# Hashed attention and a feed-forward layer on one core: projections asked for first, one key copy on VectorE, the first pair's values of one half in one stretch, features first in all its scores but one

## The chip, the cores and the metric

The kernel runs on one core of a Trainium2 chip. The metric is the device time of one execution in microseconds (us). Before the change it is 849.15 us, the median of three runs (848.68 to 849.31). Five engines work side by side, each through its own instructions in order: TensorE (PE, with its weight loads listed as PEld), VectorE (DVE), ScalarE (ACT), GpSimd (POOL) and SyncE (SP). SP and ACT also issue the DMA transfers; such issues are listed as SPq and ACTq.

## The reference

The first part is attention over 4 batches of 8 heads, 768 positions, 64 numbers per head, in which a query sees only the keys of its own hash bucket. The second is a feed-forward layer on 3072 tokens with 512 and 2048 features.

```python
q_bits = (einsum('bhsd,dk->bhsk', q, proj) > 0)      # 6 bits; the same for k
mask = q_bucket[:, :, :, None] == k_bucket[:, :, None, :]
scores = where(mask, scale * (q @ k.T), -1e9)
attn = exp(scores - max); attn = attn / (sum(attn) + 1e-9)
out = attn @ v                                       # heads side by side: x, 3072 x 512
h = x @ w_in
y = (h * sigmoid(1.702 * h)) @ w_out
```

## The kernel before, in words

The attention works through 16 pairs of heads (`pairs`, n = 0 to 15; j = 0, 1 is the head in the pair). For a pair, q and k are brought into a layout with the 64 numbers of each head on the partitions (`own`). The mask comes from a second, small product: the 6 hash bits of each key and query are turned into bf16 "features" (`feats`), whose product is large and negative wherever two bits differ. A tile of scores is 128 keys by 384 queries for both heads; it is the sum in PSUM of the f32 product of k and q and of the bf16 product of the features. ScalarE takes the exponential of the tile (`weigh`, L484) into `es`. `values` (L540) multiplies v by these tiles, with 12 matmul instructions for three key tiles and 24 for six; the trace has two records for each f32 matmul. The sums of the weights are formed on GpSimd (`add_low`, L525) and VectorE (`add_high`, L535 and L538).

The queries of a pair are in two halves (c = 0, 1) and its keys in six tiles, three `low` and three `high`. All this is written out by hand: four engines (`ORDERED`, L18) execute in the order of the source, and the fetches on SP keep their program order through `load` (L344).

Pair 0 is special. `first_pair` (L373) issues the DMAs of k, q and proj, builds the hash weights on VectorE (`hash_weights`, L126 to L136, which need proj), runs five matmuls on an idle tile, transposes k and q on PE (`turned`, L395 to L401, two query or key columns of 64 at a time), copies the results from PSUM into `own` by ScalarE or VectorE (`placed`, L403, L405), projects (`bits`, L407 to L412: a matmul at L410 and a VectorE instruction at L411 that writes the features) and leaves the second half of the features to `second` (L425), which is called as `rest()` after the first three score tiles. That second half holds the features of the keys from 384 on and of the second half of the queries. Where `second` projects, k's projection and q's stand one after the other on PE, into one PSUM tile, ahead of both VectorE instructions.

From pair 1 on q and k are fetched in another layout (`fetch`, L347), transposed by VectorE (`turn`, L432, L435), hashed in one go (`hashed`, L454, L460), and the features go from `featured` (L463, L465) by ten small DMAs of 16 rows into `feats`. From pair 2 on (`BY_PARTS`, L334) the scores are made of three terms (`scores_of_four`, L499, L514), for which `exchange` (L437) swaps partition blocks by four DMAs and `copied` (L478) repeats the features by two. `measure` (L445, L450) squares and sums q and k on ScalarE. `place` and `in_turn` (L310 to L317) hand out four PSUM places; the first pair's score tiles use three of them by the list `slots` (L620). `scores` (L486) makes the tiles of pairs 0 and 1; the order of its two terms is set at L492 and L493. The lines L614 to L651 are the hand-written order for pair 0 and the preparations of pairs 1 to 3.

After the attention the feed-forward part runs as nested products of sums of blocks (L847 to L1455); the change does not touch it.

Of the kernel before, what the change touches and what calls it, by code (L numbers as in the profile page):

```python
# [38 lines left out]
def kernel(  # L39
# [17 lines left out]
    nc = tc.nc  # L57

    loader = [nc.sync]
    B, H, S, D = q.shape  # L60
# [23 lines left out]
    pj = const.tile([P, NB], F32, name="pj")  # L84
# [25 lines left out]
    for i, x in enumerate("kq"):  # L110
# [7 lines left out]
        for c in range(2):  # L118
            r0 = D * i + 32 * c
# [41 lines left out]
    for x in (0x3FFFFFFF, 0xFF800000):  # L161
        m = const.tile([P, 1], U32, name=f"mask_{x:x}")
# [131 lines left out]
    def attention(ff):  # L294
# [4 lines left out]
        with actx:  # L299
# [10 lines left out]
            def place(i):  # L310
                return (sps if i % 4 else ends).tile([P, 2, 512], F32, tag=f"s{i % 4}", name="s")
# [32 lines left out]
            def load(out, in_):  # L344
                return tc.keep_in_program_order(nc.sync.dma_start(out=out, in_=in_))

            def fetch(n, name):  # L347

                b, hp = pairs[n]
                if n in (1, 3):  # L350

                    b1, hp1 = pairs[last - 1 - "kq".index(name)]
                    x = xT[:, hp1, b1 * S : (b1 + 1) * S].rearrange("p (s i) -> p s i", i=32)
                else:
                    x = ld.tile([P, S // 32, 32], F32, tag=name, name=name)
                raws[n, name] = x
                src = {"k": k, "q": q}[name]
                for j in range(2):
                    rows = src[b, 2 * hp + j].rearrange("(s p) (a i) -> a p s i", p=32, i=32)
                    for a in range(D // 32):  # L360
                        r0 = D * j + 32 * a
                        load(x[r0 : r0 + 32], rows[a])

            def fetch_v(n):
                b, hp = pairs[n]
                x = vts[n] = ld.tile([P, 2, T, D], F32, tag="v", name="v", bufs=2)
                heads = v[b, 2 * hp : 2 * hp + 2]
                if n:
                    load(x.rearrange("p j t d -> p (j t) d"), heads.rearrange("j (t p) d -> p (j t) d", p=P))
                else:  # L370
                    load(x.rearrange("p j t d -> p j (t d)"), heads.rearrange("j (p t) d -> p j (t d)", p=P))

            def first_pair():  # L373


                b, hp = pairs[0]
                x = {}
                for name, src, queues in (("k", k, (nc.sync, nc.scalar)), ("q", q, (nc.scalar, nc.scalar))):
                    raw = raws[0, name] = ld.tile([P, S // 32, 32], F32, tag=name, name=name)
                    x[name] = raw.rearrange("p s i -> p (s i)").rearrange("p (j t d) -> p j t d", j=2, d=D)  # L380
                    for j, queue in enumerate(queues):
                        queue.dma_start(out=x[name][:, j], in_=src[b, 2 * hp + j].rearrange("(p t) d -> p t d", p=P))
                    if name == "k":
                        for j in range(2):
                            nc.sync.dma_start(out=pj[D * j : D * (j + 1)], in_=proj)
                    xts[0, name] = own[0][:, "kq".index(name)]

                nc.scalar.activation(const.tile([1, 1], F32, name="first"), ones[0:1, 0:1], Act.Exp)
                warm = place(3)
                for _ in range(5):  # L390
                    nc.tensor.matmul(warm[:, 0], idle[:, 0:P], idle, start=True, stop=True)
                hash_weights()


                def turned(name):  # L395
                    tp = in_turn()
                    for j in range(2):
                        for i in range(GT):
                            two = x[name][:, j, 2 * i : 2 * i + 2, :].rearrange("p t d -> p (t d)")
                            nc.tensor.transpose(tp[:, j, i * P : (i + 1) * P], two, ident)  # L400
                    return tp  # L401

                def placed(name, tp, c, moves):  # L403
                    for j, move in enumerate(moves):
                        move(xts[0, name][D * j : D * (j + 1), c * HS : (c + 1) * HS], tp[D * c : D * (c + 1), j, 0:HS])  # L405

                def bits(name, c, h):  # L407
                    cols = slice(c * HS, (c + 1) * HS)
                    h = h[:, 0:HS]
                    nc.tensor.matmul(h, pf0[name].rearrange("p j d -> p (j d)"), xts[0, name][:, cols], start=True, stop=True)  # L410
                    return lambda: nc.vector.tensor_scalar(feats[0][name][:, cols], h, above0[name][:, 0:1], FEAT[name],  # L411
                                                           op0=Alu.is_gt, op1=Alu.mult)  # L412

                act, dve = nc.scalar.copy, nc.vector.tensor_copy
                tk = turned("k")
                placed("k", tk, 0, (act, act))
                tq = turned("q")
                placed("q", tq, 0, (act, dve))
                bits("k", 0, in_turn()[:, 0])()
                placed("k", tk, 1, (act, dve))  # L420
                bits("q", 0, in_turn()[:, 0])()
                placed("q", tq, 1, (act, dve))
                measure(0, "k")

                def second():  # L425
                    at = place(3)
                    for f in [bits(x, 1, at[:, i]) for i, x in enumerate("kq")]:
                        f()

                return second  # L430
# [6 lines left out]
            def exchange(n):  # L437

                for j in range(2):
                    for i in range(2):  # L440
                        r0, r1 = D * j + 32 * i, D * j + 32 * (1 - i)
                        dma = load(other[n % 3][r0 : r0 + 32], own[n % 3][r1 : r1 + 32])
                return dma

            def measure(n, name):  # L445

                x = raws[n, name]
                i = 2 * n + "kq".index(name)
                junk = xT[:, HP - 1, (B - 1) * S : B * S].rearrange("p (s i) -> p s i", i=32)
                nc.scalar.activation(junk, x, Act.Square, accum_out=sizes[:, i : i + 1])  # L450
# [35 lines left out]
            def scores(n, c, kts, slots=None):  # L486
                qT, kT, qf, kf = xts[n, "q"], xts[n, "k"], feats[n % 2]["q"], feats[n % 2]["k"]
                cols = slice(c * HS, (c + 1) * HS)
                for kt in kts:
                    ps = in_turn() if slots is None else place(slots.pop(0))  # L490
                    keys = slice(kt * P, (kt + 1) * P)
                    terms = ((kf, qf), (kT, qT))  # L492
                    for at, (a, m) in enumerate(terms if n else terms[::-1]):  # L493
                        for j in range(2):
                            hs = slice(D * j, D * (j + 1))
                            nc.tensor.matmul(ps[:, j, 0:HS], a[hs, keys], m[hs, cols], start=at == 0, stop=at == 1)  # L496
                    weigh(n, c, kt, ps)
# [42 lines left out]
            def values(n, c, kts, at):  # L540
                av, vt = at[:, 0 : HS + 1], vts[n]
                avs[n, c] = av
                for t in kts:
                    row = t if n else 2 * (t % GT) + t // GT
                    for j in range(2):
                        for d in range(0, D, 32):
                            nc.tensor.matmul(av[D * j + d : D * j + d + 32, :], vt[:, j, row, d : d + 32], es[c][:, t, j, :],  # L547
                                             start=(t == 0), stop=(t == T - 1))
# [71 lines left out]
            slots = [2, 0, 1] * 5  # L620
# [2 lines left out]
            measure(0, "q")  # L623
            fetch(2, "q")
            add_low(0, 0)
            at = place(3)
            scores(0, 0, high, slots)
            for x in "kq":
                turn(1, x)
                measure(1, x)  # L630
            values(0, 0, low, at[:, 0])
            for x in "kq":
                fetch(3, x)
            scores(0, 1, low, slots)
            add_high(0, 0)
            add_low(0, 1)
            for x in "kq":
                turn(2, x)
                measure(2, x)
            values(0, 0, high, at[:, 0])  # L640
            hashed(1, place(slots.pop(0))[:, 0])
            unload(0, 0)
            behind = exchange(2)
            whole(featured(1, behind))
            fetch_v(1)
            scores(0, 1, high, slots)
            add_high(0, 1)
            at = place(3)
            values(0, 1, every, at[:, 0])
# [807 lines left out]
    def whole(steps):  # L1457
        for _ in steps:
            pass
# [49 lines left out]
```

## Time and profile before

| | |
|---|---|
| median of three runs | 849.15 us |
| the profiled execution | 848.73 us |
| its span, first to last instruction | 846.9 us |
| PE busy | 838.0 us (99%) |
| VectorE busy | 673.8 us (80%) |
| ScalarE busy | 337.6 us (40%) |
| GpSimd busy | 366.6 us (43%) |
| score tiles of pairs 0 and 1 end | about 40 us |
| first scores of pair 2 | 45.37 us |

Instructions carry the line of the kernel that made them. A row of the timeline has the start, the length, the engine, the line, the operation, the tile written and those read, the shape and how many were merged; in brackets stand the time that the engine had been idle and what ended that. A PE row's length includes the time in which its last results drain, so rows of PE overlap; the distance from start to start is what a product costs. A waits row names the engine and line that waited, what it waited for, the total in us, how often and the longest. The row with "DMA to landing" has the least, median and greatest time from the issue of a transfer to its landing.

### The profile page before, as it was taken

How to read it: one execution, taken by the hardware profiler on the slowest of the kernel's cores; microseconds unless marked ns; L12 is line 12 of the kernel's file. 1: busy time of each engine (PE TensorE's matmuls, PEld its weight loads, DVE VectorE, ACT ScalarE, POOL GpSimd, SP SyncE). 2: the span in 40 equal slices, each digit the busy share in tenths (PEclk: the TensorE clock that was granted, in tenths of full speed). 3: DMA queues.
4: the chain of work that ended last, by engine and by line, in shares of the span. 5: the costliest groups of instructions: out<-in, count | busy, mean ns of one | idle time of the engine just before them, and what ended most of it. 6: DMA issues, size and time to landing. Idle time of an engine off the chain costs nothing.

```text
span 846.9 us, 14955 instructions
## 1 busy us (share of the span) xinstructions
PE 838.0 (99%) x5644; PEld 519.2 (61%) x5644; DVE 673.8 (80%) x1068; ACT 337.6 (40%) x552; POOL 366.6 (43%) x321
## 2 busy tenths in 40 slices
PE   8999999999999999999999999999999999999996
PEld 4444444444444444566666666545888888888885
DVE  5478888887888985788888788577998977797776
ACT  6766766767676634443444344433000000000000
POOL 4433443334344359996844487578655000000000
PEclk9999999999999999999999999999999999999999
DMA  8687666677773104345555546587754685467524
GB/s 150 117 164 159 156 132 142 141 153 148 155 158 94 50 2 173 149 170 203 218 199 193 211 174 224 198 292 265 263 192 156 193 255 193 156 199 248 197 103 101
DMA packets 165197, 144.92 MB, mean 171 GB/s; under 512 B 124224, under 2 KB 139712, under 8 KB 159872
## 3 DMA queue, kind: packets, MB, share of 16 engines
q1 hardware_dynamic: 154640, 112.11, 47.4%
q10 hardware_dynamic: 10480, 31.81, 11.1%
q8 instruction: 45, 0.74, 0.4%
q14 instruction: 32, 0.26, 0.1%
HBM read 79.69 MB, written 50.33 MB: 154 GB/s over the span
## 4 chain that ended last, share of the span: by engine, by line
PE 98%; POOL 1%; DVE 1%; ACT 0%; issue 0%; ACTq 0%; POOLq 0%; DVEq 0%
PE product L1229 30%; PE product L900 23%; PE s L547 15%; PE s L514 15%; PE small L970 6%; PE product L970 3%; PE s L496 2%; PE s L460 1%; PE s L569 1%; PE s L410 0%; POOL feat L337 0%; DVE feat L411 0%; ACT c L915 0%; DVE own L405 0%; DVE v L918 0%
## 5 line engine op out<-in xcount | busy, mean ns | idle before, releaser
L484 ACT ACTIVATE e<-s 128x768 f32<-128x768 f32 x192 | 143.4, 811 | 48.9 <-PE s L514 43.9
L547 PE MATMUL s<-e,v 128*32 128x385 f32 x1536 | 131.1, 488 | 0.0
L525 POOL TENSOR_TENSOR t_x<-e 128x768 f32<-128x768 f32 x32 | 60.5, 1891 | 136.4 <-ACT e L484 136.4
L900 PE MATMUL product<-xT,w_in_sb 128*128 128x512 f32 x216 | 100.0, 593 | 0.1
L547 PEld LDWEIGHTS s<-e,v 128*32 128x32 f32 x1536 | 46.6, 109 | 79.3 <-issue 62.2
L900 PE MATMUL product<-t_x,s_in 128*128 128x512 f32 x192 | 89.4, 592 | 0.0
L514 PE MATMUL s<-s_in 32*128 32x384 f32 x912 | 87.8, 481 | 0.0
L525 POOL TENSOR_TENSOR t_x<-t_x,e 128x768 f32<-128x768 f32 x32 | 55.2, 1724 | 43.5 <-ACT e L484 42.1
L538 DVE TENSOR_TENSOR acc<-acc,e 128x768 f32<-128x768 f32 x63 | 70.1, 1112 | 2.3
L1265 ACT COPY u<-product 128x256 f32<-128x256 f32 x20 | 7.4, 372 | 158.4 <-PE product L1229 125.2
L900 PEld LDWEIGHTS product<-xT,w_in_sb 128*128 128x128 f32 x216 | 40.9, 190 | 35.8 <-issue 32.5
L514 PEld LDWEIGHTS s<-s_in 32*128 32x128 f32 x912 | 43.8, 185 | 23.4 <-issue 2.2
L900 PEld LDWEIGHTS product<-t_x,s_in 128*128 128x128 f32 x192 | 36.5, 190 | 29.7 <-issue 26.9
L514 PE MATMUL s<-own 32*128 32x384 f32 x432 | 44.3, 482 | 0.0
L465 DVE TENSOR_SCALAR f<-s,above,weight 128x384 bf16<-128x384 f32 x15 | 10.2, 677 | 39.8 <-PE s L569 33.9
L918 DVE TENSOR_TENSOR u<-product,u 128x256 f32<-128x256 f32 (+1 forms) x60 | 28.4, 485 | 15.6 <-PE product L970 12.9
L1229 PE MATMUL product<-raw_g,xT 128*128 128x256 f32 x152 | 35.1, 379 | 0.0
L535 DVE SCALAR_TENSOR_TENSOR acc<-t_x,e 128x768 f32<-128x768 f32 x31 | 29.3, 945 | 6.3 <-POOL t_x L525 3.5
L231 POOL TENSOR_TENSOR v<-c,v 128x1024 f32<-128x1024 f32 (+1 forms) x15 | 32.4, 2159 | 1.0
L230 POOL TENSOR_TENSOR u<-v,u 128x1024 f32<-128x1024 f32 (+1 forms) x11 | 23.9, 2169 | 20.4 <-ACT v L915 15.6
L918 DVE TENSOR_TENSOR v<-product,v 128x512 f32<-128x512 f32 x24 | 16.5, 688 | 20.0 <-PE product L900 20.0
L1229 PEld LDWEIGHTS product<-raw_g,xT 128*128 128x128 f32 x152 | 28.9, 190 | 3.9
(297 smaller groups left out, 1770.7 us busy)
## 6 DMA issues: line engine op xcount, KB each, us to landing
raw_g<-g_dram SPq DMA_DIRECT2D x20, 1024.0 KB, 5.1
s_in<-g_dram SPq DMA_DIRECT2D x20, 1024.0 KB, 5.1
g_dram<-c ACTq DMA_DIRECT2D x18, 512.0 KB, 2.9
raw<-in_moe_w_out_dram ACTq DMA_DIRECT2D x16, 512.0 KB, 3.7
raw<-in_moe_w_in_dram ACTq DMA_DIRECT2D x15, 512.0 KB, 3.8
s_in<-own SPq DMA_DIRECT2D x36, 192.0 KB, 4.0
v<-in_v_dram SPq DMA_DIRECT2D x16, 384.0 KB, 4.1
k<-in_k_dram SPq DMA_DIRECT2D x52, 96.0 KB, 3.0
```

The lines of the kernel that those rows point to most:

```text
L230: return [lambda: eng.tensor_tensor(t1, b12, b11, op=Alu.subtract), lambda: eng.tensor_tensor(b12, b22, b12, op=Alu.subtract), lambda: eng ...
L231: lambda: eng.tensor_tensor(b12, b22, b12, op=Alu.subtract),
L484: nc.scalar.activation(es[c][:, kt, :, 0:HS], ps[:, :, 0:HS], Act.Exp, scale=1.0 / D**0.5)
L514: nc.tensor.matmul(ps[i][:, j, 0:HS], a[r0 : r0 + 32, keys], m[r0 : r0 + 32, cols], start=at == 0, stop=at == 2)
L525: nc.gpsimd.tensor_tensor(low_sum, low_sum if i else e[:, 0], e[:, i + 1], op=Alu.add)
L535: nc.vector.scalar_tensor_tensor(acc, terms[0], T * TINY, terms[1], op0=Alu.add, op1=Alu.add)
L538: nc.vector.tensor_tensor(acc, acc, terms[i + 1], op=Alu.add)
L547: nc.tensor.matmul(av[D * j + d : D * j + d + 32, :], vt[:, j, row, d : d + 32], es[c][:, t, j, :], start=(t == 0), stop=(t == T - 1))
L900: nc.tensor.matmul(ps, wq[LEFT[i]][:, kc, :], xq[RIGHT[i]][:, kc, :], start=(start and kc == 0), stop=(kc == K2 - 1), skip_group_check=not ...
L918: nc.vector.tensor_tensor(dst, x, y, op=Alu.add)
L970: nc.tensor.matmul(x, wq[LEFT[i]], xq[RIGHT[i]], start=start, stop=True, skip_group_check=True)
L1229: nc.tensor.matmul(ps, wq[LEFT[i]][:, c, :], gq[RIGHT[i]][:, c, :], start=(onto is None and c == 0), stop=(c == F4 - 1), skip_group_check= ...
```

## The change

1. The two DMAs of `proj` become the first that SP issues. Both halves of k and the first of q are issued by ACT, the second of q by SP behind the projections. (Before: SP had one half of k and then the projections, ACT the other half of k and all of q.)
2. Of the first copies of k from PSUM (keys below 384), VectorE makes the one of the second head; ScalarE made both.
3. In pair 0 the bf16 product of the features comes ahead of the f32 product in every tile but the first. Before, it came behind in all of pair 0. Pair 1 had it in front already.
4. The values of the first query half are computed in one stretch of six key tiles, behind the first three score tiles of the second query half; before, in two stretches of three.
5. Measures and fetches move accordingly: pair 1's measures and pair 2's k measure behind those three score tiles, pair 2's q measure behind the last three. On SP the order becomes k of pair 3, pair 1's features, q of pair 3, v of pair 1, the exchange of pair 2; before, k and q of pair 3, the exchange, the features, v.

```diff
@@ fetch
-                        load(x[r0 : r0 + 32], rows[a])
+                        dma = load(x[r0 : r0 + 32], rows[a])
+                return dma
@@ first_pair
-                for name, src, queues in (("k", k, (nc.sync, nc.scalar)), ("q", q, (nc.scalar, nc.scalar))):
+                for j in range(2):
+                    nc.sync.dma_start(out=pj[D * j : D * (j + 1)], in_=proj)
+                for name, src, queues in (("k", k, (nc.scalar, nc.scalar)), ("q", q, (nc.scalar, nc.sync))):
...
-                    if name == "k":
-                        for j in range(2):
-                            nc.sync.dma_start(out=pj[D * j : D * (j + 1)], in_=proj)
...
-                placed("k", tk, 0, (act, act))
+                placed("k", tk, 0, (act, dve))
@@ scores
-                    for at, (a, m) in enumerate(terms if n else terms[::-1]):
+                    for at, (a, m) in enumerate(terms if n or c or kt else terms[::-1]):
@@ the order of pair 0
-            at = place(3)
             scores(0, 0, high, slots)
             for x in "kq":
                 turn(1, x)
-                measure(1, x)
-            values(0, 0, low, at[:, 0])
-            for x in "kq":
-                fetch(3, x)
             scores(0, 1, low, slots)
             add_high(0, 0)
             add_low(0, 1)
             for x in "kq":
                 turn(2, x)
-                measure(2, x)
-            values(0, 0, high, at[:, 0])
+                measure(1, x)
+            measure(2, "k")
+            behind = fetch(3, "k")
+            at = place(3)
+            values(0, 0, every, at[:, 0])
             hashed(1, place(slots.pop(0))[:, 0])
             unload(0, 0)
-            behind = exchange(2)
             whole(featured(1, behind))
+            scores(0, 1, high, slots)
+            measure(2, "q")
+            fetch(3, "q")
             fetch_v(1)
-            scores(0, 1, high, slots)
+            exchange(2)
             add_high(0, 1)
```

## The prediction

> **What bounds the kernel now.** I read the page's part 1 first, then the waits of PE, then the timeline of the first 50 us, engine by engine. Times are us from the span's start.
>
> ```profile
> span 846.9 us, 14955 instructions
> ...
> PE 838.0 (99%) x5644; PEld 519.2 (61%) x5644; DVE 673.8 (80%) x1068; ACT 337.6 (40%) x552; POOL 366.6 (43%) x321
> ```
>
> TensorE is busy 99% of the span; no other engine comes near. Its waits, all of them:
>
> ```profile
> PE s L391 <- DVE idle L76: 1.3, 1, 1.3
> PE s L410 <- POOL above L339: 0.4, 1, 0.4
> PE s L410 <- ACT own L405: 0.2, 1, 0.2
> PE s L400 <- DMA k<-in_k_dram: 0.2, 1, 0.2
> ```
>
> That is 2.1 us, all before 8 us. So an edit counts by what it does to the moment at which PE passes a point, and what another engine does counts only where PE waits for it. The span is 846.9 and the profiled run 848.73, so 1.83 lies around the span. I make the sum against 848.73; the median of the three runs is 849.15, 0.42 more, and what I find is added to that median. About 0.2% (1.7 us) is what a measurement of this kernel can tell from no change, and that is nearly all the waiting that PE does.
>
> **The change part by part.** The order of each engine's instructions in the two kernels differs only ahead of pair 2's scores (45.4 us in the trace of now); behind that it is the same. There are five places.
>
> *The start.* First the queues.
>
> ```profile
> 0.74 0.40 SPq L382 DMA_DIRECT2D k<-in_k_dram  x1
> 0.83 0.39 ACTq L382 DMA_DIRECT2D k<-in_k_dram  x1
> ...
> 1.20 1.20 SPq L385 DMA_DIRECT2D pj<-in_proj_dram  x2
> ```
>
> SP will issue the projections at 0.74 and 1.3 (now 1.2 and 1.8) and the second q at 1.9; its next fetches stay at about 2.4. ACT issues both k, from 0.83 on, and the first q, 0.4 apart, so the second k goes out 0.4 later than now.
>
> ```profile
> 3.79 1.51 PE L400 MATMUL s<-ident,k 128*128 128x128 f32 x6 [0.21 <-DMA k<-in_k_dram]
> ...
> 5.10 1.09 PE L400 MATMUL s<-ident,q 128*128 128x128 f32 x6
> ...
> 5.34 1.95 ACT L405 COPY own<-s 64x384 f32<-64x384 f32 x4 [1.63 <-PE s L400]
> ...
> 5.74 0.24 DVE L133 SCALAR_TENSOR_TENSOR pf_k<-pj,ones 64x6 f32<-64x6 f32 x2 [0.53 <-DMA pj<-in_proj_dram]
> ...
> 6.41 0.88 PE L410 MATMUL s<-own,pf_k 128*128 128x384 f32 x2 [0.23 <-ACT own L405]
> ...
> 6.98 0.55 DVE L405 COPY own<-s 64x384 f32<-64x384 f32 x1
> ...
> 8.80 0.62 DVE L411 TENSOR_SCALAR feat<-s,above_q 128x384 bf16<-128x384 f32 x1
> ...
> 9.47 0.34 PE L496 MATMUL s<-feat 64*128 64x384 bf16 x2
> ```
>
> DVE sets PE's first bf16 product at 9.47: from 6.98 it goes through copy, k features, copy and q features without a stop (2.44), and the product follows their end at 9.42. Ahead of 6.98 stand the hash weights, 1.24 from the second projection's landing (5.74). The edit puts one more copy (0.55) behind these weights, and PE's k projection (6.41) will wait for it instead of for ACT's second copy. Step by step: the transposes of k begin 0.1 later (the second half lands later) and end at 5.4; ACT copies half of the keys by 5.9 (its four copies take 1.95, so 0.49 each); DVE copies the other half from 5.95 to 6.5, if its weights are done by then; PE projects from 6.6 to 7.5 (0.88); k features until 8.15, the copy until 8.7, q features until 9.35. PE's bf16 product stands at 9.4 instead of 9.47: about 0. It needs the weights by 5.95, so the second projection by 4.7.
>
> ```profile
> pj<-in_proj_dram SPq DMA_DIRECT2D x2, 1.5 KB, 3.8
> ```
> ```profile
> DMA to landing us min/median/max: 1.7/2.5/5.6
> ```
>
> Bounds: with the 3.8 of now it lands at 5.1, the weights end at 6.4, and all of DVE's chain slides by 0.5. The last row is that of the feature copies between 20 and 75 us, small like the projections: 1.7 to 5.6 from issue to landing, 2.5 in the median; the projections of now have half of k ahead of them on their own queue. Ahead of everything, with 2.5, the second lands at 3.8. I take this end, being nearest in size: **0.0**, and keep 0.5 as the other. Below nothing there is at most 0.1, since nothing moves the transposes forward.
> The Trainium skill (DMA: Bandwidth & Descriptors, Anatomy of one DMA) gives a transfer a fixed cost of about 2.0 us, fitted on GpSimd's path. By it the second projection would land near 3.3, an estimate, and this term would be 0.0; by the row of 3.8 it would be +0.5. The row of now speaks against that page's figure, the 1.7 for it.
>
> *Features first in the fourth tile.*
>
> ```profile
> 12.88 0.92 PE L496 MATMUL s<-own 64*128 64x384 f32 x4
> ...
> 12.99 0.62 DVE L411 TENSOR_SCALAR feat<-s,above_k 128x384 bf16<-128x384 f32 x1 [2.98 <-PE s L410]
> ...
> 13.66 0.34 PE L496 MATMUL s<-feat 64*128 64x384 bf16 x2
> ...
> 13.84 0.81 PE L496 MATMUL s<-own 64*128 64x384 f32 x4
> ```
> ```profile
> 31.08 0.33 PE L496 MATMUL s<-feat 64*128 64x384 bf16 x2
> ...
> 31.89 0.33 PE L496 MATMUL s<-feat 64*128 64x384 bf16 x2
> ```
>
> The keys from 384 up get their features from the second pair of projections, which ends just before 12.99; DVE then needs 0.62, to 13.61. Now PE covers this with the tile's f32 products (from 12.88), and at 13.66 only the bf16 product is left: the next tile starts at 13.84. In the new order the bf16 product, which waits for DVE, stands in front, and as PE works in order everything behind it waits too: the f32 products of this tile, and all later tiles. From 13.66 the whole tile is still to do, 0.81 (31.08 to 31.89, where features are first), until 14.47: **+0.63**. The other tiles have their features by then: the second and third use those that the first waited for, and those of the second query half, one more 0.62 on DVE, are needed two us later.
>
> *Values in one stretch.*
>
> ```profile
> 15.29 0.33 PE L496 MATMUL s<-feat 64*128 64x384 bf16 x2
> ...
> 18.37 0.33 PE L496 MATMUL s<-feat 64*128 64x384 bf16 x2
> ...
> 22.21 0.49 PE L460 MATMUL s<-own,pf_k 128*32 128x384 f32 x2
> ...
> 23.88 0.81 PE L496 MATMUL s<-own 64*128 64x384 f32 x4
> ...
> 25.59 4.09 PE L547 MATMUL s<-e,v 128*32 128x385 f32 x48
> ...
> 29.50 0.49 PE L460 MATMUL s<-s_in,pf_k 128*32 128x384 f32 x2
> ```
>
> Between the bf16 products at 15.29 and 18.37 lie 3.08, with the first half of the values in them. Of these, 0.81 is a tile and 1.95 the values (half of the long stretch, 25.59 to 29.50); the remaining 0.32 is the price of changing over to values and back. That goes: **-0.32**. ACT then has six exponentials in a row, as long as PE's tiles, so three score buffers carry them.
>
> *Features first behind the hash.* Hash and one tile with own first take 22.21 to 23.88, 1.67; with features first, in pair 1, 29.50 to 31.08, 1.58: **-0.09**.
>
> *ACT and the queues.*
>
> ```profile
> 17.32 0.84 ACT L450 ACTIVATE xT<-xT 128x768 f32<-128x768 f32 x1
> ```
>
> Three measures, some 1 each with their reading, move behind the six exponentials, ahead of the first unload. That unload waits for the 3.9 of values anyway, so the values hide them; uncovered they would push the exponentials behind, and PE's second values, by up to 3. The last measure moves to where ACT idles. On SP the q fetch of pair 3 and the exchange of pair 2 move behind pair 1's feature copies, ahead of pair 2's:
>
> ```profile
> 19.84 2.19 SPq L345 DMA_DIRECT2D xT<-in_q_dram  x4
> 22.13 2.59 SPq L345 DMA_DIRECT2D s_in<-s_in  x4
> 24.84 4.33 SPq L345 DMA_DIRECT2D feat<-f  x6
> 29.21 0.58 SPq L345 DMA_DIRECT2D v<-in_v_dram  x1
> 31.10 4.94 SPq L345 DMA_DIRECT2D feat<-f  x8
> ...
> 38.57 1.14 SPq L345 DMA_DIRECT2D feat<-feat  x2
> ...
> 46.22 6.52 SPq L345 DMA_DIRECT2D feat<-f  x8
> ```
> ```profile
> 45.37 0.34 PE L514 MATMUL s<-feat 32*128 32x384 bf16 x4
> ```
>
> Pair 1's copies can start at 24.1, when their source is written, and end at 28.4; with 2.2 + 0.6 + 2.6 behind them pair 2's start at 33.9, 2.8 later than now. The two last copies are then issued by 42.5 and land (2.5) at 45.0; PE reads them at 45.6. **0**, with half a us to spare. Pair 3's fetches, behind these, are later too, and are used a pair later.
>
> **Sum:** 0.0 + 0.63 - 0.32 - 0.09 = +0.22. 848.73 + 0.22 = 848.95; on the median, 849.4.
>
> **The rivals.**
> - *Projections land as long after their issue as now*: DVE's chain slides by 0.5 and PE with it: 849.9. For it: the 3.8. Against: what was ahead of them is gone.
> - *The fourth tile does not wait*, and the change brings what its parts take away: -0.41, so 848.7. For it: only k's features are needed there. Against: DVE waited for PE until 12.99, though k's projection is the earlier of the two, so nothing lets it start sooner.
> - *SP is late for pair 2.* With an exchange straight ahead of them, pair 3's eight copies took 6.52 and not 4.94. Pair 2's would then have their last copies landed at 46.6, and PE, there at 45.6, stands for up to 1.0: 849.9 to 850.4, I take 850.2. It decides once the copies take 0.5 more. Against: pair 3's ring also carried fetches of weights.
> - *TensorE's pace falls back*, the case on the slow side, at the wait of the fourth tile. Six transposes of k took 1.51 from 3.79, six of q 1.09 from 5.10: PE began slow, and sped up in the second six, some 4 after its first matmul (1.3). The new wait leaves PE 0.7 to 0.9 without work before 13.66; if that sent it back, half of another such stretch is lost, 2.1: 851.5. It decides at the length of that gap. Against: the gaps of 0.2 and 0.4 among PE's waits sent nothing back.
> The Trainium skill (TensorE: Matmul & The Clock Gate, What's actually happening) lets the clock halve after an idle window of about 3.4 us; by it this gap is harmless. No wait of PE in this trace is longer than 1.3.
>
> **How the numbers follow.** Likeliest, 0.55: 849.4. Late projections, 0.17: 849.9. No wait, 0.10: 848.7. SP, 0.12: 850.2. Clock, 0.06: 851.5. The range runs from 848.4 (no wait, less 0.3) to 850.4 (SP at its worst); 0.3 is about how far the runs of now lie from their median. It leaves out the clock and the edges. Faster by over 0.2% is below 847.5, slower above 850.8, which only the clock reaches: 0.02, 0.92, 0.06.
>
> **What would show it.** The second projection lands before 4.7 and DVE's added copy starts near 5.95; PE's first bf16 product is near 9.4; PE stands 0.7 to 0.9 between the second projections and a bf16 product that follows DVE's L411; one stretch of 48 value products stands where two of 24 stood; pair 2's first product comes 0.1 to 0.4 later than 45.37. A wait of PE for a DMA at pair 2, or slow matmuls behind 13 us, would make the prediction wrong.

## The result and the profile after

The changed kernel takes **853.55 us** (median of 6 runs, 851.40 to 853.99), the kernel before 849.19 in the same comparison (848.68 to 849.44): a ratio of 1.0047, 95% interval 1.0034 to 1.0060. So it is slower by 4.4 us; the forecast was 849.4, and the range ended at 850.4. The profiled execution took 852.55.

The head and part 1 of the profile's page, for after:

```profile
span 850.7 us, 14951 instructions
...
PE 838.7 (99%) x5644; PEld 519.1 (61%) x5644; DVE 677.8 (80%) x1069; ACT 337.5 (40%) x551; POOL 367.4 (43%) x321
```

The span grew by 3.8 and PE's work by 0.7. The rest is waiting. All of PE's waits in after (waited for, total us, times, longest):

```profile
PE s L514 <- DMA feat<-feat: 1.5, 1, 1.5
PE s L391 <- DVE idle L76: 1.3, 1, 1.3
PE s L400 <- DMA q<-in_q_dram: 1.1, 1, 1.1
PE s L496 <- DVE feat L411: 0.7, 1, 0.7
PE s L410 <- POOL above L339: 0.2, 1, 0.2
```

Three are new: 1.1 for q, 0.7 for DVE at the fourth tile, 1.5 for the feature copies of pair 2. Only the second was in the forecast. PE's timeline in after, at the places that the prediction quotes of before:

```profile
3.47 1.51 PE L400 MATMUL s<-ident,k 128*128 128x128 f32 x6
6.12 0.98 PE L400 MATMUL s<-ident,q 128*128 128x128 f32 x6 [1.14 <-DMA q<-in_q_dram]
...
10.19 0.50 PE L496 MATMUL s<-feat 64*128 64x384 bf16 x4
...
14.34 0.34 PE L496 MATMUL s<-feat 64*128 64x384 bf16 x2 [0.71 <-DVE feat L411]
...
15.16 0.33 PE L496 MATMUL s<-feat 64*128 64x384 bf16 x2
...
26.48 4.09 PE L547 MATMUL s<-e,v 128*32 128x385 f32 x48
...
46.26 0.34 PE L514 MATMUL s<-feat 32*128 32x384 bf16 x2
48.07 0.50 PE L514 MATMUL s<-feat 32*128 32x384 bf16 x2 [1.48 <-DMA feat<-feat]
48.25 1.62 PE L514 MATMUL s<-s_in 32*128 32x384 f32 x16
```

Of before one row is needed besides, the same first exchanged product of pair 2:

```profile
45.54 1.46 PE L514 MATMUL s<-s_in 32*128 32x384 f32 x16
```

The transposes of k start 0.3 earlier than before, those of q 1.0 later. Start against start, after is late by 0.72 at the first bf16 product (10.19, 9.47), by 1.32 at the fifth tile (15.16, 13.84), by 0.89 at the second values (26.48, 25.59), by 0.89 at pair 2's first product (46.26, 45.37), by 2.71 at its first exchanged one (48.25, 45.54), and by 3.8 at the end. The differences are the terms of the sum:

| term | forecast | in the trace |
|---|---|---|
| start | 0.0 | +0.72 |
| fourth tile | +0.63 | +0.60 |
| values and hash | -0.41 | -0.43 |
| wait at pair 2 | 0 | +1.82 |
| from there to the end | 0 | +1.1 |

These are the terms of the profiled execution (852.55 against 848.73); the median of after lies 1.0 above it. Two terms hold nearly to the last digit. The miss lies in the start, in the wait at pair 2 and behind that. What is lost behind it comes in small steps: by the same products after is 2.87 late at 103.79 (before: 100.92), 3.52 at 398.10 (394.58), in a part of the kernel that the change does not touch, and 3.8 at the end.

**The start.** The DMA issues between 1.7 and 2.1 us, with the median time to landing, in after:

```profile
q<-in_q_dram ACTq DMA_DIRECT2D x1, 192.0 KB, 4.3
q<-in_q_dram SPq DMA_DIRECT2D x1, 192.0 KB, 4.5
pj<-in_proj_dram SPq DMA_DIRECT2D x1, 1.5 KB, 4.0
```

and of q in the same view of before:

```profile
q<-in_q_dram ACTq DMA_DIRECT2D x2, 192.0 KB, 3.5
```

The second projection, with only the first ahead of it on its queue, took 4.0 and not the 2.5 that I chose; q took 4.3 to 4.5 in place of 3.5, and its halves were issued 0.3 to 0.5 later. DVE in after:

```profile
5.41 0.24 DVE L133 SCALAR_TENSOR_TENSOR pf_k<-pj,ones 64x6 f32<-64x6 f32 x2 [1.56 <-DMA pj<-in_proj_dram]
...
6.65 0.55 DVE L405 COPY own<-s 64x384 f32<-64x384 f32 x1
```

The weights start 0.33 earlier than before (5.74), not 1.9, so the added copy starts at 6.65 and not at 5.95.

**SP.** Its timeline in after:

```profile
21.07 2.02 SPq L345 DMA_DIRECT2D xT<-in_k_dram  x4
24.83 3.74 SPq L345 DMA_DIRECT2D feat<-f  x6
28.67 4.02 SPq L345 DMA_DIRECT2D xT<-in_q_dram  x4
32.73 0.53 SPq L345 DMA_DIRECT2D v<-in_v_dram  x1
33.31 3.45 SPq L345 DMA_DIRECT2D s_in<-s_in  x4
36.85 5.14 SPq L345 DMA_DIRECT2D feat<-f  x8
...
44.42 1.15 SPq L345 DMA_DIRECT2D feat<-feat  x2
...
62.15 1.27 SPq L345 DMA_DIRECT2D feat<-feat  x2
```

Pair 1's features end at 28.57, near the 28.4 of the prediction. Then the queries, v and the exchange took 8.1 where I put 5.4 (their lengths before): 4.02 for 2.2 and 3.45 for 2.6. Pair 2's features start at 36.85 instead of 33.9, and the copies land at 48.1 and not at 45.0.

### The profile page after: what moved, and what is told of

It reads as the page before. It is cut to its first block, busy times and chain, and to the rows that moved or that the text cites. A ratio compares the mean times of both kernels' runs of the same rounds, so it can differ in the third digit from the quotient of the medians.

```text
span 850.7 us, 14951 instructions
## 1 busy us (share of the span) xinstructions
PE 838.7 (99%) x5644; PEld 519.1 (61%) x5644; DVE 677.8 (80%) x1069; ACT 337.5 (40%) x551; POOL 367.4 (43%) x321
## 4 chain that ended last, share of the span: by engine, by line
PE 97%; POOL 1%; SPq 0%; DMA 0%; DVE 0%; issue 0%; ACT 0%; ACTq 0%; POOLq 0%
PE product L1229 30%; PE product L900 23%; PE s L514 15%; PE s L547 15%; PE small L970 6%; PE product L970 3%; PE s L496 2%; PE s L460 1%; PE s L569 1%; SPq L345 0%; DMA feat<-feat 0%; PE s L410 0%; DVE feat L411 0%; POOL feat L337 0%; ACT c L915 0%
## 5 line engine op out<-in xcount | busy, mean ns | idle before, releaser
L918 DVE TENSOR_TENSOR u<-product,u 128x256 f32<-128x256 f32 (+1 forms) x60 | 28.4, 485 | 15.5 <-PE product L970 12.5
L514 PEld LDWEIGHTS <-feat 32*128 32x128 bf16 x336 | 10.0, 92 | 35.7 <-issue 23.5
```

The lines of the kernel that those rows point to most:

```text
L514: nc.tensor.matmul(ps[i][:, j, 0:HS], a[r0 : r0 + 32, keys], m[r0 : r0 + 32, cols], start=at == 0, stop=at == 2)
L918: nc.vector.tensor_tensor(dst, x, y, op=Alu.add)
```

## The experiments

All are set against runs of the kernel before on the same chip (848.86, 849.01 and 849.09 in the three groups). Lines in their rows are those of each kernel. An interval that holds 1 can't be told from no change.

| run | median (range), us | against before | ratio, 95% interval |
|---|---|---|---|
| start_only | 850.47 (849.17-851.35) | +1.61 | 1.0016, 1.0007-1.0025 |
| feat_only | 849.47 (849.21-849.73) | +0.61 | 1.0006, 0.9997-1.0015 |
| order_only | 851.48 (850.59-852.14) | +2.62 | 1.0030, 1.0018-1.0043 |
| copies_first | 853.04 (851.35-853.50) | +4.18 | 1.0043, 1.0029-1.0056 |
| proj_only | 851.78 (851.46-852.53) | +2.77 | 1.0033, 1.0021-1.0045 |
| q_on_act | 850.27 (849.53-851.21) | +1.26 | 1.0015, 1.0006-1.0024 |
| values_only | 848.75 (848.39-849.21) | -0.26 | 0.9998, 0.9989-1.0007 |
| values_feat | 848.54 (848.25-848.92) | -0.47 | 0.9994, 0.9985-1.0003 |
| proj_behind | 849.41 (848.83-850.37) | +0.32 | 1.0007, 0.9998-1.0016 |
| gate_fill | 849.82 (849.29-850.18) | +0.73 | 1.0009, 1.0000-1.0018 |
| sp_moved | 851.42 (850.53-852.07) | +2.33 | 1.0026, 1.0015-1.0036 |
| measures_moved | 849.83 (849.65-851.03) | +0.74 | 1.0011, 1.0002-1.0020 |

**The change in three parts.** The start alone (parts 1 and 2):

```diff
+                for j in range(2):
+                    nc.sync.dma_start(out=pj[D * j : D * (j + 1)], in_=proj)
-                ... (("k", k, (nc.sync, nc.scalar)), ("q", q, (nc.scalar, nc.scalar))):
+                ... (("k", k, (nc.scalar, nc.scalar)), ("q", q, (nc.scalar, nc.sync))):
...
-                    if name == "k":
-                        for j in range(2):
-                            nc.sync.dma_start(out=pj[D * j : D * (j + 1)], in_=proj)
...
-                placed("k", tk, 0, (act, act))
+                placed("k", tk, 0, (act, dve))
```

> The kernel before with parts 1 and 2 of the change alone (projections first, k on ScalarE's queue, the second q on SyncE's, one key copy on VectorE). If the start loses what the profile of the changed kernel shows at its third score tile (0.7 us at 11 us, from q landing late), this run takes 849.9 and its q lands near 6 us. If that late landing was an accident of one profile, it takes 849.2.

Features first alone (part 3):

```diff
-                    for at, (a, m) in enumerate(terms if n else terms[::-1]):
+                    for at, (a, m) in enumerate(terms if n or c or kt else terms[::-1]):
```

> The kernel before with part 3 alone (features first in all score tiles of the first pair but one). By the wait of the fourth tile for VectorE (0.63) less two cheaper changes of matmul shape (0.09 each): 849.6. If the fourth tile's wait is made up later, 849.0.

The order of pair 0 alone (parts 4 and 5, the last hunk of the diff of the change):

> The kernel before with parts 4 and 5 alone (values in one stretch, measures, fetches and exchange moved). Theory: SyncE falls some 5 us behind and the copied features of the second pair come late, so TensorE waits there 1 to 2 us and again later, less 0.3 for the values: 851 to 852. Rival: the long landing at 48 us was a collision with a transfer of program code (16 KB at 45.9 us) in one execution and not the order's doing: 848.9.

The three come to +4.84, the whole to +4.36: the loss is there in the parts, and within the intervals they add up. Features first are 0.61 above before in the median, which the interval can't tell from nothing; PE's fourth tile in that run has the forecast wait all the same:

```profile
13.96 0.34 PE L496 MATMUL s<-feat 64*128 64x384 bf16 x2 [0.71 <-DVE feat L411]
```

The order, from which I expected a gain of 0.32, costs 2.62, and PE waits at pair 2 as in after. From PE's timeline:

```profile
46.69 0.65 PE L515 MATMUL s<-feat 32*128 32x384 bf16 x2 [1.12 <-DMA feat<-feat]
```

**Values in one stretch, without the moved transfers and measures**, then the same with features first in all tiles of pair 0 but the first and the fourth:

```diff
-            at = place(3)
             scores(0, 0, high, slots)
...
-            values(0, 0, low, at[:, 0])
...
-            values(0, 0, high, at[:, 0])
+            at = place(3)
+            values(0, 0, every, at[:, 0])
```
```diff
-                    for at, (a, m) in enumerate(terms if n else terms[::-1]):
+                    for at, (a, m) in enumerate(terms if n or c or kt not in (0, GT) else terms[::-1]):
```

> The kernel before with the values of the first half in one stretch, and ScalarE's and SyncE's order left as it was. Theory: the lateness of SyncE comes from moving measures, fetches and exchange, not from the values: TensorE waits for no feature repeats, and the two changes of matmul shape that go bring 0.3: 848.6. Rival: the later values or exponentials themselves delay what SyncE needs: 849.5 or more.

> As the run with the values alone, and features first in the first pair's tiles except the first and the fourth, which keep the f32 product in front. Theory: the fourth tile's wait for VectorE is what features first cost, so leaving it out brings two cheaper changes of matmul shape (0.09 each): 848.4. Rival: another tile waits for its features: 849 or more.

The medians are -0.26 and -0.47, with intervals that also hold no change at all. The sizes are what the working gave (-0.32; -0.41), too small to be proven here. The second has the lowest median of all kernels run, 0.47 below before. So the stretch of values isn't what costs.

**What of the order costs.** SP's transfers moved as in the change, the measures left:

```diff
-            at = place(3)
...
                 turn(1, x)
                 measure(1, x)
-            values(0, 0, low, at[:, 0])
-            for x in "kq":
-                fetch(3, x)
...
-            values(0, 0, high, at[:, 0])
+            behind = fetch(3, "k")
+            at = place(3)
+            values(0, 0, every, at[:, 0])
...
-            behind = exchange(2)
             whole(featured(1, behind))
-            fetch_v(1)
             scores(0, 1, high, slots)
+            fetch(3, "q")
+            fetch_v(1)
+            exchange(2)
```

and the counterpart, with the measures moved and the exchange left ahead of pair 1's features:

```diff
-            at = place(3)
...
                 turn(1, x)
-                measure(1, x)
-            values(0, 0, low, at[:, 0])
-            for x in "kq":
-                fetch(3, x)
...
                 turn(2, x)
-                measure(2, x)
-            values(0, 0, high, at[:, 0])
+                measure(1, x)
+            measure(2, "k")
+            for x in "kq":
+                fetch(3, x)
+            at = place(3)
+            values(0, 0, every, at[:, 0])
...
             scores(0, 1, high, slots)
+            measure(2, "q")
```

> The kernel before, with the first pair's values in one stretch and SyncE's transfers in the order of the change (the keys of pair 3 behind the second turn, the queries of pair 3, v and the exchange of pair 2 behind the features of pair 1), but ScalarE's measures where they were. Theory (SyncE reaches the features of pair 2 too late because what stands ahead of them is more than it gets issued in that time): the copies feat<-feat of pair 2 land at 46.5 us or later, TensorE waits 1 us or more for them, and the time is 850.4 to 851.5. Rival (the measures on ScalarE are what holds SyncE): the copies land by 45.5, and the time is 848.5 to 849.2.

> The counterpart: the kernel before, with the first pair's values in one stretch and ScalarE's measures where the change puts them (both of pair 1 behind the second turn, that of pair 2's queries behind the scores), and the fetch of pair 3 only so much later as these measures force; the exchange of pair 2 stays ahead of the features of pair 1. Theory (SyncE's order is the cost, not the measures): SyncE has time left ahead of the features of pair 2, their copies land by 45.5 us, and the time is 848.5 to 849.4. Rival (the later measure, which the fetch of pair 3 waits for, is the cost): 850.4 to 851.5.

sp_moved, timelines of SP and of PE:

```profile
27.37 2.23 SPq L345 DMA_DIRECT2D xT<-in_q_dram  x4
29.64 1.59 SPq L345 DMA_DIRECT2D v<-in_v_dram  x1
31.28 3.44 SPq L345 DMA_DIRECT2D s_in<-s_in  x4
34.82 5.01 SPq L345 DMA_DIRECT2D feat<-f  x8
...
42.26 1.14 SPq L345 DMA_DIRECT2D feat<-feat  x2
```
```profile
46.46 0.33 PE L515 MATMUL s<-feat 32*128 32x384 bf16 x1 [1.08 <-DMA feat<-feat]
```

measures_moved, the same two:

```profile
26.97 4.29 SPq L345 DMA_DIRECT2D feat<-f  x6
...
40.11 1.15 SPq L345 DMA_DIRECT2D feat<-feat  x2
```
```profile
31.03 0.49 PE L497 MATMUL s<-feat 64*128 64x384 bf16 x2 [0.47 <-issue]
```

With SP's order alone the fetch of pair 3's keys starts where it did before (17.33), and all the same PE waits 1.08 at pair 2 and the time is +2.33, nearly all of the +2.62 of the order. In values_only the stretch of values costs nothing that can be measured; that the copies land late through SP's order alone is shown. With the measures alone the copies are issued at 40.1 and PE doesn't wait for them, but 0.74 is lost, more than theory allowed (849.4): PE stands 0.5 at the first tile of pair 1, whose features SP now starts at 26.97 instead of 24.84, behind an exchange that is itself behind the later fetch. The profile names no releaser for that wait, but the times fit: SP's first feature copy, issued at 26.97, landed 4.0 later, at about 31.0, and PE goes on at 31.03.

**Is it enough to put pair 2's copies ahead?** The changed kernel with the two copies issued ahead of the fetch that stands in front of them:

```diff
             whole(featured(2))
+            copied(2)
             fetch(4, "k")
             scores_of_four(1, ((0, 0), (0, 2), (0, 4)))
             add_low(1, 0)
-            copied(2)
             fetch(4, "q")
```

> The changed kernel, with the two feature repeats of the second pair issued ahead of the key fetch of the fourth instead of behind it. Theory of the late SyncE: TensorE's wait at the second pair (1.5 us) goes; some of it may come back at the third pair, whose repeats then come later: 852.0, and 853.3 if all of it comes back. Rival (an accident of one execution): the same as the changed kernel.

The wait for the copies went, and the time hardly moved: +4.18 against the +4.36 of the change, a difference that these runs can't tell from nothing. PE waits 1.0 at pair 3 in its place:

```profile
59.67 1.49 DVE L186 SCALAR_TENSOR_TENSOR w_in_sb<-raw,mask_3fffffff 128x512 uint32<-128x512 uint32 x1 [1.61 <-DMA raw<-in_moe_w_in_dram]
...
63.49 0.58 ACT L559 ACTIVATE xT<-s,vs 128x384 f32<-128x384 f32 x1
...
64.12 0.34 PE L514 MATMUL s<-feat 32*128 32x384 bf16 x2 [1.01 <-ACT xT L559]
```
```profile
64.39 1.15 SPq L345 DMA_DIRECT2D feat<-feat  x2
```

That wait is not one for copies of features: pair 3's are issued at 64.39, when PE has gone on. The rows lead back to a fetch of weights on ACT's queue (`raw`, 512 KB). DVE waited 1.61 for it, ACT 2.93 for DVE, and PE 1.01 for ACT. The fetch took 7.8 from issue to landing, 7.8 in order_only and 8.1 in sp_moved too, where DVE waited 0.6 and 0.9 for it; it took 5.7 in before and 5.5 to 7.0 in the runs that leave SP's order alone or move the measures only. In after it took 6.0, with SP's new order, so that SP's later transfers hold it up is an argument, not shown.

SP is no earlier afterwards: pair 3's copies are issued at 64.39, in after at 62.15, and before in

```profile
56.52 1.14 SPq L345 DMA_DIRECT2D feat<-feat  x2
```

In the profiled execution of copies_first 1.9 had been lost by 41.94 (in after 0.9 by 40.94; both are the start of pair 1's last values, 40.05 in before), and 2.5 were lost behind that, against 2.9 in after. So taking away the wait at pair 2, 1.8 long, brought 0.4; most of it is lost again behind, at another wait.

**What of the start costs.** First the projections alone at the head of SP's queue, everything else as before; then the start of the change with both halves of q on ScalarE:

```diff
+                for j in range(2):
+                    nc.sync.dma_start(out=pj[D * j : D * (j + 1)], in_=proj)
                 for name, src, queues in (("k", k, (nc.sync, nc.scalar)), ("q", q, (nc.scalar, nc.scalar))):
...
-                    if name == "k":
-                        for j in range(2):
-                            nc.sync.dma_start(out=pj[D * j : D * (j + 1)], in_=proj)
```
```diff
-                ... (("k", k, (nc.scalar, nc.scalar)), ("q", q, (nc.scalar, nc.sync))):
+                ... (("k", k, (nc.scalar, nc.scalar)), ("q", q, (nc.scalar, nc.scalar))):
```

> The kernel before with the two projections ahead of the k half on SyncE's queue and nothing else. Theory: q is slow because its halves travel on both queues, the second beside the small packets of the next pair, and the projections do no harm: q lands by 5.5 us, 849.0. Rival: transfers of 24-byte pieces at the head slow what comes behind: q lands after 6 us, 849.9 to 850.5.

> The start of the changed kernel (projections first, k on ScalarE's queue, one key copy on VectorE), but both halves of q on ScalarE's queue; the rest as before the change. Theory of the two queues: q lands by 5.6 us and the run takes 849.0. Rival of the projections: q lands after 6 us, 850.4.

The second diff is set against the start of the change. The projections alone cost the most of all starts, 2.77, more than their rival allowed (850.5). The half of k behind them on SP's queue took

```profile
k<-in_k_dram SPq DMA_DIRECT2D x1, 192.0 KB, 4.5
```

from its issue at 2.0, so to 6.5, where in before it took 2.9 from 0.74: of the 2.9 by which it lands later, 1.3 are the later issue and 1.6 the longer landing. The first half of q, issued at 1.28 on ACT's queue, still landed after 2.6; the second, issued at about 1.7, after 4.4. PE's first transposes (whose wait the profile puts down to POOL, though the landing is 0.1 ahead of them) began at

```profile
6.62 1.51 PE L399 MATMUL s<-ident,k 128*128 128x128 f32 x6 [3.03 <-POOL above L339]
```

And with SP's queue free of q the start still costs 1.26. My theory that the spread of q over two queues was the matter falls. The opposite edit keeps the queues of the change, with the projections behind SP's half of q, and both first copies on ScalarE:

```diff
-                ... (("k", k, (nc.sync, nc.scalar)), ("q", q, (nc.scalar, nc.scalar))):
+                ... (("k", k, (nc.scalar, nc.scalar)), ("q", q, (nc.scalar, nc.sync))):
...
+                for j in range(2):
+                    nc.sync.dma_start(out=pj[D * j : D * (j + 1)], in_=proj)
                 nc.scalar.activation(const.tile([1, 1], F32, name="first"), ones[0:1, 0:1], Act.Exp)
```

> The kernel before, with the queues of the change (both halves of k and the first of q asked for by ScalarE, the second half of q by SyncE), but with the two projections behind q's half on SyncE; ScalarE makes both copies of the first keys as before. Theory (what stands behind the projections at the head of the queues comes late, whoever asks for it): q's halves land at 4.6 to 5.5 us again instead of 5.8 to 7.0, TensorE doesn't wait more than 0.5 us for q, and the time is 848.8 to 849.4. Rival (three transfers of 192 KB on ScalarE's queue and one on SyncE's are the cost): one half of q lands at 6 us or later, TensorE waits over 1 us for it, and the time is 849.9 to 850.5.

The issues of its first 2 us, to landing:

```profile
k<-in_k_dram ACTq DMA_DIRECT2D x2, 192.0 KB, 3.3
q<-in_q_dram SPq DMA_DIRECT2D x1, 192.0 KB, 2.9
q<-in_q_dram ACTq DMA_DIRECT2D x1, 192.0 KB, 3.6
pj<-in_proj_dram SPq DMA_DIRECT2D x2, 1.5 KB, 3.7
```

All four large transfers take as long again as in before (2.9 to 3.7), and the difference in time is no longer one that can be measured (+0.32). This profile is that of the fastest of 11 executions, though; five of them took 850.06 to 850.37, and what those lost no trace shows. The two runs together say that it is the projections' place that costs: proj_only moves nothing else and costs 2.77. (proj_behind also gives the key copy back to ScalarE; no run has that copy alone.)

Other traffic does not explain the late q. ACT's third transfer, a half of q issued at 1.73 in proj_behind and at 1.75 in after, took 3.6 and 4.3. Between 3 and 4 us ACT's queue moved 0.36 MB in proj_behind and 0.33 in before, but 0.25 in after and 0.17 in start_only, and all queues together 0.37, 0.35, 0.28 and 0.19. With the projections first less was moved at that time, not more.

The last run keeps the late q and takes away only TensorE's idling:

```diff
                 tk = turned("k")
                 placed("k", tk, 0, (act, dve))
+                for _ in range(4):
+                    nc.tensor.matmul(warm[:, 1], idle[:, 0:P], idle, start=True, stop=True)
                 tq = turned("q")
```

> Parts 1 and 2 of the change alone, with four more products of zeros (128x512, bf16, 0.46 us each before the clock is granted) between k's transposes and q's, where TensorE waited 1.7 us for q. Theory (a good part of the lost 1.6 us is that TensorE's first steps ran at half pace longer, because it idled while q landed): q lands as late as before but the transposes after it and the first scores run at full pace, and the time is 849.2 to 849.7, a microsecond less than without the four. Rival (only q's and the second projection's landings count): 850.3 to 850.7 again; if the four products stand in the way themselves, 851.

PE in start_only:

```profile
6.76 1.54 PE L399 MATMUL s<-ident,q 128*128 128x128 f32 x6 [1.70 <-DMA q<-in_q_dram]
8.10 1.49 PE L409 MATMUL s<-own,pf_k 128*128 128x384 f32 x2
...
10.95 0.92 PE L495 MATMUL s<-own 64*128 64x384 f32 x4
```

and in gate_fill:

```profile
6.23 0.94 PE L399 MATMUL s<-ident,q 128*128 128x128 f32 x6
7.41 0.89 PE L409 MATMUL s<-own,pf_k 128*128 128x384 f32 x2 [0.23 <-POOL above L339]
...
9.23 0.92 PE L497 MATMUL s<-own 64*128 64x384 f32 x4
```

From q's first transpose to the first tile start_only needs 4.19 and gate_fill 3.00, with the same instructions. In start_only one projection follows the other after 1.45 (8.10 to 9.55), and the second pair's after 0.75 (13.72 to 14.47). So the transposes and the projections run at half pace where PE had idled 1.7, and at full pace where four idle products filled that time. The profiled execution of start_only is one of its slow ones (851.21); the medians differ by 0.88 (+1.61 and +0.73), close to the theory, and nine of start_only's eleven executions lie further above before than any of gate_fill's. What stays, 0.73 with an interval that begins at no change, fits the late q and the late second projection, which gate_fill keeps (4.4 to 4.6, and 4.1): the same as the 0.72 in the trace of after, whose own profiled run had its pace by then (q's six transposes in 0.98).
The Trainium skill (TensorE: Matmul & The Clock Gate, What's actually happening) says that the array runs at half clock until one window of about 3.4 us has been busy, and that the windows run freely, so that the turning point differs from run to run. The two traces fit that, and so does the spread of the start kernels: 2.2 us from lowest to highest for start_only, 0.9 for gate_fill. The column of the granted clock shows 1.00 in all these stretches; the pace is read from the lengths of the rows and the distances between them.

## Why the prediction was wrong

- **Start: wrong.** The step that failed is "ahead of everything, with 2.5, the second lands at 3.8". I took the price from feature copies of another stretch and 3.8 as the far end; the second projection took 4.0. The step also treated the projections as free for what follows them. The two halves of q took up to 1.0 longer each, PE waited 1.1 for them, and my end of +0.5 had no such term. In its place: 0.7 for the landings, and about 0.9 more, in the median of the start alone, for the half pace that PE's wait for q prolongs. That "nothing moves the transposes forward" was wrong too, without harm: those of k began 0.3 earlier. The rival of the late projections had the direction, and 0.5 where the trace has 0.7 and the median 1.6.
The Trainium skill (DMA: Bandwidth & Descriptors, Anatomy of one DMA) would have had the second projection land near 3.3, an estimate. Here it landed at about 5.4, where the hash weights begin (5.41); it took 4.0 in after and 3.9 in before. The page fits its figure on GpSimd's path; for these transfers of SyncE's the measurement decides against it.
- **Fourth tile: right.** +0.63 forecast, +0.60 in the trace, with PE's wait of 0.7 where it was said to be; the median of feat_only, +0.61, is too small to prove it. The rival in which that tile doesn't wait is out.
- **Values and hash: right** in size, -0.41 against -0.43 in the trace; one stretch of 48 products stands from 19.29, as forecast. The runs alone could not resolve it.
- **Queues: wrong.** The step that failed is "with 2.2 + 0.6 + 2.6 behind them pair 2's start at 33.9". I carried lengths of issues from one place in SP's order to another. The three took 8.1 in after, 7.4 in sp_moved; 2.7 late against half a us to spare, and the copies themselves landed 3.4 after their issue in the median, not 2.5. The rival named the wait, but it got 0.12, and a price of at most 1.0 that ended with the first wait: that wait cost 1.8, and another 1.1 goes behind it. My reason against the rival does not hold either: the weights that I had in mind travel on ACT's queue (issued at 47.16), not on SP's. And before's own slowest rows ahead of 60 us, 3.49 for such a fetch and 3.13 for an exchange, would have warned.
- **ACT: half right.** The unload was covered, as I said. What I didn't follow is that the fetch of pair 3's keys overwrites what the moved measure reads: SP waited 5.1 for that measure, its issue went from 17.32 to 21.07, and the measures alone cost 0.74.
- **Pace: named at the wrong place.** Behind the fourth tile's wait the rows stay at 0.81, as before. The pace was lost at the start, at the wait for q that I did not see.
- The range was too narrow because I bounded both wrong terms from rows of other places and let 0.5 and 1.0 be their ends.

Open are: why two transfers of 1.5 KB at the head delay what is behind them on both queues; why SP's three issues take longer in the new place (DMA engines that are busy are the likeliest, not tested); and what causes the last 1.1 of after, which is spread over waits too short for the views. In the other profiled executions with SP's new order that part is 0.4 (order_only) and 2.1 (sp_moved).

## What to carry to other kernels

The length of an issue row belongs to its place: when transfers are put in another order on a queue, bound them by the slowest such rows in the trace, and where a queue has no pause afterwards, follow the delay to every later user and not only to the first. A small transfer at the head of a queue need not be free for the large ones behind it. Where PE starts at half pace, a wait of a microsecond or two can cost more than its length, since the half pace can last longer; a few idle products in it are worth trying.

## What the runs showed of the hardware

- In after the second projection, 1.5 KB, took 4.0 from issue to landing, and the two halves of k issued beside it on the other queue, 192 KB each, 2.5 in the median. In the six kernels with the projections first, transfers of 192 KB issued by 1.3 took 2.4 to 2.6, and those issued from 1.7 on 4.1 to 5.1; in proj_behind those issued from 0.74 to 1.73 took 2.9 to 3.6.
- Four exchanges took 3.45 to issue in after and 2.59 before; four fetches of 96 KB 4.02 and 2.19.
- In start_only a projection at 8.10 still ran at half pace (1.49; the next begins 1.45 later, against 0.75 in the second pair of projections), though PE had been busy from 1.3 on but for one wait of 1.7.
